# An mLSTM cell and a SwiGLU block in one kernel: first weights loaded earlier, words joined in place, and steps of the first group moved

## The chip, the cores and the metric

The kernel runs on one core of one Trainium2 chip. The metric is the device time of one launch in microseconds; the figure compared is the median of the timed runs. Block, piece and slot numbers count from 0.

## What is computed

The reference runs an mLSTM recurrence over 4 batches, 8 heads, 768 steps and head size 40, lays the heads of a token side by side, and puts the 3072 tokens of 320 values through a SwiGLU block with 1536 hidden values:

```python
for t in range(S):
    m_new = np.maximum(f_gate[:, :, t] + m, i_gate[:, :, t])
    f_stab = np.exp(f_gate[:, :, t] + m - m_new)
    i_stab = np.exp(i_gate[:, :, t] - m_new)
    C = f_stab * C + i_stab * outer(v_t, k_t)
    n = f_stab * n + i_stab * k_t
    y[:, :, t] = sigmoid(o_gate_t) * (C @ q_t) / max(|n . q_t|, 1)
x = y.transpose(0, 2, 1, 3).reshape(B * S, H * D)
g = x @ w_gate
out = (g * sigmoid(g) * (x @ w_val)) @ w_out
```

Inputs are float32, except that the three weight matrices come as float64 and are turned into float32 words on the chip.

## The kernel before

**Groups.** The 768 steps are cut into six groups of 128, for all 32 heads at once. For each group the recurrence is done in its chunked form (scores of q and k, weighed by gate factors, plus a state carried from 64 steps to 64 steps), and its 512 token rows (4 batches of 128) then go through the block: twelve hidden blocks of 128 values (`hidden`, L594 to L605, ten float32 matmuls each, into two PSUM banks of the tag "gen"; ScalarE takes the Silu of one, VectorE multiplies by the other), then the output projection (`project_all`, L618, for group 0, `project`, L612, for the others).

**The order is written out by hand.** The kernel runs under a manual schedule: each engine executes its instructions in the order in which the code emits them. The recurrence of group n+1 is put between the hidden blocks of group n, by the table `slots` (L671 for group 0) and, for group 0, the table `after` (L689) between the twelve steps of the projection. A slot's functions are emitted after the hidden block with its number.

**The first group** (L520 to L562) is done ahead of everything, in one piece of 128 steps per head: gate factors by matmuls into PSUM (`first_mask`, `first_inputs`, `first_maxima`), transposes of k and q (`first_turn`), scores, `first_own` and `first_x` per batch, `first_gate` (times the sigmoid of the output gates, `sig`), `first_seam` (transposes of the token rows, then copies into `xT`), `first_state`. Heads come in two halves, P = 0 and 1. `burn` (L422) issues matmuls on constant data whose result nobody reads.

**Weights.** `PIECES` cuts them into ten pieces: 0 and 1 hold hidden blocks 0 and 1, pieces 2 to 6 two hidden blocks each, pieces 7 to 9 the output matrix. `piece_load` (L136) loads the words of w_gate into partitions 0 to 63 through SP's queue (the gate half) and those of w_val into partitions 64 to 127 through ScalarE's queue (the val half). Pieces 0, 1, 4 and 5 share two buffers `raw`; pieces 2 and 6 use the end of `h_sb`, piece 3 the space of `wo_sb`. `convert(j)` (L206) makes float32 words of block j in three steps: `scale` (two ScalarE multiplications, into `top` and `low`), `join` (two VectorE operations, into `both`), `rounded` (an integer add of `both` and `low` into the weights' place, on GpSimd or VectorE). `top`, `low` and `both` have one buffer each. `ahead` (L668) says which block is converted behind which hidden block: m+2 behind m.

**Queues.** SP issues nearly all loads, ScalarE the first gate rows (L127, L129, L130) and the val halves. A transfer waits on its issuing engine for the buffers that it writes, and for the earlier transfer whose completion semaphore it takes over: eight such semaphores go round in the order of issue. What stands behind it on that engine waits too.

**Gate factors of the later groups.** `late_sums` and `late_maxima` (L271, L278) scan all later steps at once, `decay_rows` and `decay` prepare the decay factors, `late_turns` transposes the gate rows; `late_maxima` also writes `M_dram`, which `weights_load` (L400) spreads into `w_sb`. For a group `weights_sub`, `weights_mask` (GpSimd) and `weights_exp` make the factors, `do_scores` and `do_weigh` the weighed scores, `do_add` and `do_state` the two new states, `do_attend` and `do_gather` the outputs, `do_divide` and `seam` the rows for the block.

**PSUM.** Two tags of four banks each go round: "gen" (`first_y`, hidden blocks, projection) and "cell" (all else, the burns among it). A new tile waits until the readers of the bank's last tile are done.

Of the kernel before, what the change touches and what calls it, by code (L numbers as in the profile page):

```python
# [11 lines left out]
I32 = mybir.dt.int32  # L12
U32 = mybir.dt.uint32
AF = mybir.ActivationFunctionType
ALU = mybir.AluOpType
# [3 lines left out]
L = 128  # L19
# [5 lines left out]
def kernel(  # L25
# [18 lines left out]
    nc = tc.nc  # L44
# [12 lines left out]
    NKC = DM // HP  # L57
    UH = BH // 2
    UA = UH // 2
    NH = NFC + 1  # L60
# [10 lines left out]
    conv = early_scope.enter_context(tc.tile_pool(name="conv", bufs=2))  # L71

    def flat(t):
        return t.rearrange("p c t -> p (c t)")

    def bank(name, tag="cell"):
        return psum.tile([128, 512], F32, name=name, tag=tag)
# [7 lines left out]
    k_sb = const.tile([128, BH, DP], F32)  # L85
    q_sb = const.tile([128, BH, DP], F32)
    v_sb = const.tile([128, BH, D1], F32)
    o_sb = const.tile([128, BH, D], F32)
# [9 lines left out]
    h_sb = const.tile([128, NH, TW], F32)  # L98
# [7 lines left out]
    f_sb = early.tile([BH, NS - 2, SUB], F32)  # L106
    i_sb = early.tile([BH, NS - 2, SUB], F32)
# [4 lines left out]
    def load(dst, a, c, P):  # L112
        nc.sync.dma_start(out=dst[:, heads(P), 0:D], in_=tokens(a, c, P))
# [7 lines left out]
    def gate_rows(a):  # L121
        return a.rearrange("b h s -> (b h) s")
# [3 lines left out]

    nc.scalar.dma_start(out=f0, in_=spread_rows(f_gate))  # L127
    nc.sync.dma_start(out=i0, in_=spread_rows(i_gate))
    nc.scalar.dma_start(out=flat(f_sb), in_=gate_rows(f_gate)[:, L:])  # L129
    nc.scalar.dma_start(out=flat(i_sb), in_=gate_rows(i_gate)[:, L:])  # L130


    raws = {}
# [2 lines left out]
    def piece_load(p, home=None):  # L136
        kind, m, n = PIECES[p]
        if kind == "gv":
            a, d = NKC, n * 128
            src = [(slice(i * HP, (i + 1) * HP), w[:, m * 128:(m + n) * 128].rearrange("(c p) f -> p c f", p=HP))  # L140
                   for i, w in enumerate((moe_w_gate, moe_w_val))]
            queues = (nc.sync, nc.scalar)
        else:
            a, d = n, DM
            src = [(slice(0, 128), moe_w_out[m * 128:(m + n) * 128].rearrange("(a p) d -> p a d", p=128))]
            queues = (nc.sync,)
        if src[0][1].dtype == F32:
            for r, w in src:
                if kind == "o":
                    nc.sync.dma_start(out=wo_sb[r, m:m + n, :], in_=w)  # L150
                else:
                    for x in range(n):
                        nc.sync.dma_start(out=wgv_sb[r, m + x], in_=w[:, :, ts(x, 128)])
            return
        if home is None:
            raw = conv.tile([128, 4 * NKC * 128], U32, name="raw")
        else:
            raw = home.rearrange("p a t -> p (a t)").bitcast(U32)
        raw = raw[:, 0:2 * a * d]
        for (r, w), queue in zip(src, queues):  # L160
            queue.dma_start(out=raw[r].rearrange("p (a d) -> p a d", a=a), in_=w.bitcast(U32))
        words = raw.rearrange("p (a d two) -> p a d two", two=2, a=a)
        raws[p] = (words[:, :, :, 0], words[:, :, :, 1])
        split(p)


    blocks = {}
# [13 lines left out]
    def scale(j):  # L181
        if j in blocks:
            lo, hi, dst = blocks[j]
            a, d = hi.shape[1], hi.shape[2]
            top = conv.tile([128, NKC * 128], F32, name="top", bufs=1).rearrange("p (a d) -> p a d", a=a)
            nc.scalar.mul(top, hi.bitcast(F32), 2.0 ** -112)  # L186
            low = conv.tile([128, NKC * 128], I32, name="low", bufs=1).rearrange("p (a d) -> p a d", a=a)
            nc.scalar.mul(low, lo, 2.0 ** -29)
            blocks[j] = (low, top.bitcast(U32), dst)

    def join(j):
        if j in blocks:
            lo, top, dst = blocks[j]
            a = dst.shape[1]
            both = conv.tile([128, NKC * 128], U32, name="both", bufs=1).rearrange("p (a d) -> p a d", a=a)
            nc.vector.tensor_scalar(both, top, scalar1=3, scalar2=None, op0=ALU.logical_shift_left)  # L196
            nc.vector.scalar_tensor_tensor(both, in0=top, scalar=0x80000000, in1=both, op0=ALU.bitwise_and,  # L197
                                           op1=ALU.bitwise_or)
            blocks[j] = (lo, both, dst)

    def rounded(j, eng=None):
        if j in blocks:
            lo, both, dst = blocks.pop(j)
            (eng or nc.gpsimd).tensor_tensor(dst.bitcast(I32), both.bitcast(I32), lo, op=ALU.add)  # L204

    def convert(j, eng=None):  # L206
        scale(j)
# [5 lines left out]
        load(q_sb, q, 0, P)  # L213
        load(v_sb, v, 0, P)
    load(o_sb, o_gate, 0, 0)
    load(o_sb, o_gate, 0, 1)


    junk = early.tile([128, 512], BF16)
# [198 lines left out]
    def sig(P):  # L418
        nc.scalar.activation(o_sb[:, heads(P)], o_sb[:, heads(P)], AF.Sigmoid)


    def burn(n):  # L422
        t = bank("burn")
        for _ in range(n):
            nc.tensor.matmul(t, lhsT=junk[:, 0:128], rhs=junk, start=True, stop=True)  # L425

# [3 lines left out]
    A, V, G = nc.scalar, nc.vector, nc.gpsimd  # L430
# [52 lines left out]
    def first_own(u):  # L483
        first_y[u] = bank("first_y", "gen")[:, 0:H * D1].rearrange("p (h d) -> p h d", d=D1)
        for h in range(H):
            nc.tensor.matmul(first_y[u][:, h, :], lhsT=W0[:, u * H + h, :], rhs=v_sb[:, u * H + h, :], start=True, stop=True)  # L486

    def first_x(u):
        y = first_y.pop(u)
        den = work.tile([128, UH, 1], F32, name="den")[:, 0:H]  # L490
        nc.vector.tensor_scalar(den, y[:, :, D:], scalar1=1.0, scalar2=None, op0=ALU.max)
        nc.vector.scalar_tensor_tensor(den, in0=y[:, :, D:], scalar=-1.0, in1=den, op0=ALU.mult, op1=ALU.max)
        nc.vector.reciprocal(den, den)
        nc.vector.tensor_tensor(x_sb[:, u, 0:DM].rearrange("p (h d) -> p h d", d=D), y[:, :, 0:D],
                                den.to_broadcast([128, H, D]), op=ALU.mult)

    def first_gate(P):
        for u in (2 * P, 2 * P + 1):
            x = x_sb[:, u, 0:DM].rearrange("p (h d) -> p h d", d=D)
            nc.vector.tensor_tensor(x, x, o_sb[:, u * H:(u + 1) * H], op=ALU.mult)  # L500
        nc.gpsimd.tensor_copy(x_sb[:, 2 * P:2 * P + 2, DM:], x_sb[:, 2 * P:2 * P + 2, 0:HP])
# [9 lines left out]
    def first_seam(P, engs):  # L511
        for c, eng in zip(range(0, NKC, 2), engs):
            cs = range(c, min(c + 2, NKC))
            tp = bank("tp_x")[:, 0:len(cs) * 2 * L].rearrange("p (c u s) -> p c u s", u=2, s=L)
            for w in cs:
                for b in range(2):
                    nc.tensor.transpose(tp[:, w - c, b, :], x_sb[:, 2 * P + b, ds(PAIRS[w][0] * HP, 2 * HP)], ident)  # L517
            copy(eng, xT(0)[:, c:c + len(cs), 2 * P * L:(2 * P + 2) * L].rearrange("p c (u s) -> p c u s", u=2), tp)
# [14 lines left out]
    first_x(0)  # L533
    first_turn(1, q_sb, qT, (A, V))
    piece_load(0)
    piece_load(1)
    first_own(1)
    first_values(1)
    first_x(1)
    first_scores(1)  # L540
    sig(0)
    sig(1)
    piece_load(2, h_sb[:, NH - NKC:])
    piece_load(3, wo_sb)
    burn(3)
    first_own(2)
    first_own(3)
    first_gate(0)
    first_x(2)
    first_x(3)  # L550
    first_gate(1)
    first_seam(0, (A, V, A))
    scale(0)
    piece_load(4)
    burn(5)
    join(0)
    first_seam(1, (A, A, A))
    rounded(0, V)
    first_state(0, A)
    convert(1)  # L560
    piece_load(5)
# [98 lines left out]
    def load_all(dst, a, n):  # L660
        for P in range(2):
            load(dst, a, n, P)

    run = lambda f, *a: (lambda: f(*a))
# [4 lines left out]
    ahead[8] = [10, 11]  # L669
    ahead[9] = []  # L670
    slots = {  # L671
        0: [run(first_state, 1, A), run(load_all, k_sb, k, 1), run(load_all, q_sb, q, 1), run(late_maxima)],
        1: [run(decay_rows), run(piece_load, 6, h_sb[:, NH - NKC:])],
        2: [run(late_turns), run(weights_load, 1)],
        3: [run(decay), run(load_all, v_sb, v, 1)],
        6: [run(turn, 0, (A, A), (A, V)), run(piece_load, 7)],
        7: [run(turn, 1, (A, A), (A, V)), run(weights_sub, 1, 0), run(weights_sub, 1, 1), run(weights_mask, 0),
            run(weights_mask, 1)],
        8: [run(weights_exp, 0), run(weights_exp, 1), run(weigh_values, G, 0), run(weigh_values, G, 1),
            run(piece_load, 8)],  # L680
        9: [run(do_scores), run(do_weigh, 0), run(load_all, o_sb, o_gate, 1)],
        10: [run(do_weigh, 1), run(do_add), run(do_state, 2, 0), run(do_state, 2, 1)],
        11: [run(do_attend, 1, 0), run(do_gather, 1, 0, False), run(piece_load, 9)],
    }
    for m in range(NFC):
# [26 lines left out]
    for g in range(1, NG):  # L712
        n, f = g + 1, g + 2
# [64 lines left out]
```

## Time and profile before

| | |
|---|---|
| timed runs, us | 577.21, 577.31, 579.02; median 577.31 |
| the profiled execution, us | 579.26 |
| its span, us | 577.5 |
| mean granted TensorE clock | 0.993 |
| TensorE busy, us | 567.9 |
| hidden blocks (L599), busy us | 322.2 in 1440 records |
| VectorE, ScalarE, GpSimd busy, us | 211.7, 151.0, 102.4 |
| moved by DMA, MB | 37.85 |

The profile is of one execution. A float32 matmul is recorded as two passes, so a hidden block of ten matmuls shows as x20. A view by lines gives groups of instructions with their mean duration; the timeline gives start, length, engine, line, tile and, in brackets, the engine's idle time before it with what released it; the chain of waits is followed back from the last instruction of a window; a view by stretches gives busy time per engine, then the granted clock, the share of the DMA engines and GB/s. Matmuls are pipelined and their ends modelled, so a wait inside a row of matmuls can show as a longer row. L numbers are lines of the kernel before.

### The profile page before, as it was taken

What the parts mean: (1) busy time and instruction counts of PE and PEld (TensorE: products, weight loads), DVE (VectorE), ACT (ScalarE), POOL (GpSimd) and SP (SyncE); (2) the same over time, 40 slices, a digit from 0 to 9 for tenths busy, and PEclk for the clock granted to TensorE, in tenths of its full rate; (3) what the DMA queues carried; (4) which work ended last, traced back from release to release, by engine and by line L of the source; (5) the groups of instructions that cost most, each with busy time, mean ns of one, the idle gap of its engine ahead of it and who ended that gap; (6) DMA issues with size and microseconds to landing.
All of it is one profiled execution on the core that took longest, in us unless ns stands there. A gap on an engine that the chain in (4) does not pass through costs nothing.

```text
span 577.5 us, 12169 instructions
## 1 busy us (share of the span) xinstructions
PE 567.9 (98%) x5407; PEld 332.0 (57%) x5407; DVE 211.7 (37%) x378; ACT 151.0 (26%) x237; POOL 102.4 (18%) x101
## 2 busy tenths in 40 slices
PE   9998998999999999999999999999999999999997
PEld 4955454765655676455576555567555567544475
DVE  5776595860325600234620224630223630011100
ACT  3366554427210223201115210114311010011100
POOL 2132345463001141001132001232001110000000
PEclk9999998999999999999999999999999999999999
DMA  9999992494141800313620304450000000000000
GB/s 126 182 283 175 177 252 93 86 148 93 25 48 24 144 23 24 47 24 48 112 43 33 48 1 56 78 92 23 12 2 2 3 1 24 23 1 0 1 23 23
DMA packets 129915, 37.85 MB, mean 66 GB/s; under 512 B 120424, under 2 KB 125032, under 8 KB 129864
## 3 DMA queue, kind: packets, MB, share of 16 engines
q1 hardware_dynamic: 127284, 32.92, 33.0%
q10 hardware_dynamic: 2580, 4.16, 3.3%
q8 instruction: 42, 0.69, 0.5%
q14 instruction: 9, 0.07, 0.0%
HBM read 33.06 MB, written 4.01 MB: 64 GB/s over the span
## 4 chain that ended last, share of the span: by engine, by line
PE 91%; DMA 3%; ACT 3%; DVE 1%; issue 1%; POOL 0%; ACTq 0%; DVEq 0%; POOLq 0%
PE gv_ps L599 49%; PE o_ps L615 23%; PE o_ps L622 4%; DMA raw<-in_moe_w_val_dram 3%; PE inter L349 2%; PE intra L354 2%; PE add L330 2%; PE tp_kq L294 1%; PE sp L309 1%; PE first_y L486 1%; PE tp_x L395 1%; PE burn L425 1%; PE tp_x L517 1%; PE tp_kq L465 1%; PE sp L475 1%
## 5 line engine op out<-in xcount | busy, mean ns | idle before, releaser
L599 PE MATMUL gv_ps<-xT,wgv_sb 64*128 64x512 f32 x1440 | 322.2, 596 | 1.8 <-POOL wgv_sb L204 1.8
L599 PEld LDWEIGHTS gv_ps<-xT,wgv_sb 64*128 64x128 f32 x1440 | 139.6, 188 | 154.9 <-issue 150.2
L605 DVE TENSOR_TENSOR h_sb<-sg,gv_ps 128x512 f32<-128x512 f32 x72 | 49.5, 687 | 302.5 <-ACT sg L604 287.3
L615 PE MATMUL o_ps<-wo_sb,h_sb 128*128 128x320 f32 x480 | 130.5, 433 | 0.0
L615 PEld LDWEIGHTS o_ps<-wo_sb,h_sb 128*128 128x128 f32 x480 | 90.8, 190 | 38.2 <-issue 0.8
L604 ACT ACTIVATE sg<-gv_ps 128x512 f32<-128x512 f32 x72 | 43.0, 598 | 262.2 <-PE gv_ps L599 262.1
L339 POOL TENSOR_TENSOR C<-C,dec 128x328 f32<-128x328 f32 x20 | 14.5, 737 | 164.0 <-DVE C L341 164.0
L609 ACT COPY z_sb<-o_ps 128x320 f32<-128x320 f32 x24 | 10.2, 426 | 114.1 <-PE o_ps L615 102.7
L412 POOL TENSOR_SCALAR_AFFINE_SELECT w_sb<-w_sb 64x1024 f32<-64x1024 f32 x20 | 28.2, 1408 | 27.0 <-DVE w_sb L407 26.0
L622 PE MATMUL o_ps<-wo_sb,h_sb 128*128 128x320 f32 x96 | 26.9, 437 | 0.0
L375 POOL TENSOR_TENSOR o_sb<-o_sb,y_sb 128x640 f32<-128x640 f32 x10 | 14.2, 1428 | 48.6 <-DVE y_sb L366 48.6
L622 PEld LDWEIGHTS o_ps<-wo_sb,h_sb 128*128 128x128 f32 x96 | 17.9, 190 | 7.2
L366 DVE TENSOR_TENSOR y_sb<-y_sb,intra 64x328 f32<-64x328 f32 x40 | 19.7, 493 | 1.1
L319 POOL TENSOR_TENSOR vw_sb<-v_sb,w_sb 128x656 f32<-128x656 f32 x10 | 12.8, 1305 | 32.2 <-issue 32.2
L204 POOL TENSOR_TENSOR wgv_sb<-both,low 128x640 int32<-128x640 int32 x8 | 13.4, 1670 | 25.4 <-DVE both L197 25.4
L197 DVE SCALAR_TENSOR_TENSOR both<-top,both 128x640 uint32<-128x640 uint32 x18 | 15.7, 871 | 0.6
L349 PEld LDWEIGHTS inter<-C,qT 64*64 64x64 f32 x640 | 10.2, 134 | 7.3 <-issue 6.8
L196 DVE TENSOR_SCALAR both<-top 128x640 uint32<-128x640 uint32 x18 | 10.5, 581 | 9.3 <-ACT top L186 7.4
L330 PEld LDWEIGHTS add<-vw_sb,k_sb 64*64 64x64 f32 x640 | 10.5, 136 | 5.7 <-issue 4.9
L341 DVE TENSOR_TENSOR C<-C,add 128x328 f32<-128x328 f32 x20 | 9.9, 494 | 9.5 <-POOL C L339 9.3
L204 POOL TENSOR_TENSOR wo_sb<-both,low 128x640 int32<-128x640 int32 x6 | 10.2, 1700 | 17.4 <-DVE both L197 13.9
L407 DVE TENSOR_TENSOR w_sb<-g_T,w_sb 128x1024 f32<-128x1024 f32 x10 | 13.1, 1349 | 0.0
(120 smaller groups left out, 385.1 us busy)
## 6 DMA issues: line engine op xcount, KB each, us to landing
w_sb<-M_dram SPq DMA_DIRECT2D x10, 512.0 KB, 6.5
k_sb<-in_k_dram SPq DMA_DIRECT2D x12, 320.0 KB, 6.4
q_sb<-in_q_dram SPq DMA_DIRECT2D x12, 320.0 KB, 4.0
v_sb<-in_v_dram SPq DMA_DIRECT2D x12, 320.0 KB, 6.1
o_sb<-in_o_gate_dram SPq DMA_DIRECT2D x12, 320.0 KB, 6.8
raw<-in_moe_w_out_dram SPq DMA_DIRECT2D x3, 1280.0 KB, 7.2
out_dram<-z_sb SPq DMA_DIRECT2D x24, 160.0 KB, 1.8
h_sb<-in_moe_w_gate_dram SPq DMA_DIRECT2D x2, 640.0 KB, 9.0
```

The source lines that it names most:

```text
L197: nc.vector.scalar_tensor_tensor(both, in0=top, scalar=0x80000000, in1=both, op0=ALU.bitwise_and, op1=ALU.bitwise_or)
L204: (eng or nc.gpsimd).tensor_tensor(dst.bitcast(I32), both.bitcast(I32), lo, op=ALU.add)
L330: nc.tensor.matmul(ps[i][half(two), a, :], lhsT=k_sb[half(i), h, :], rhs=vw_sb[half(i), h, :], start=True, stop=True)
L339: nc.gpsimd.tensor_tensor(state(s + 1)[:, a], state(s)[:, a], dec[:, s - 2, a].unsqueeze(2).to_broadcast([128, UA, D1]), op=ALU.mult)
L349: nc.tensor.matmul(inter[two][half(i), a, :], lhsT=qT[half(two), P * UA + a, half(i)], rhs=state(2 * n + i)[half(two), P * UA + a, :], sta ...
L366: nc.vector.tensor_tensor(t, t, intra[i][half(c)], op=ALU.add)
L412: nc.gpsimd.affine_select(w, w, compare_op=ALU.is_ge, fill=NEG, base=0, pattern=[[0, UH], [1, SUB]], channel_multiplier=-1)
L599: nc.tensor.matmul(ps[i], lhsT=wgv_sb[half(i), m, PAIRS[kc][i], :], rhs=x[half(i), kc, :], start=(kc == 0), stop=(kc == NKC - 1))
L604: nc.scalar.activation(sg, ps[0], AF.Silu)
L605: nc.vector.tensor_tensor(hid(g, m), sg, ps[1], op=ALU.mult)
L615: nc.tensor.matmul(p, lhsT=hid(g, m)[:, ts(u, L)], rhs=wo_sb[:, m, :], start=(m == 0), stop=(m == NFC - 1))
L622: nc.tensor.matmul(ps[u], lhsT=hid(g, m)[:, ts(u, L)], rhs=wo_sb[:, m, :], start=(m == 0), stop=(m == NFC - 1))
```

## The change

- The rows of the later gates (`f_sb`, `i_sb`) are no longer loaded at the start, but on ScalarE's queue behind pieces 0 and 1.
- The second half of the first output gates (`o_sb`) is loaded behind piece 0 and not ahead of it.
- `join` writes its words into the weights' own place and `rounded` adds there; the tile `both` is gone, and `low` has two buffers.
- Block 0 is converted earlier and in three places: `scale` between the two sigmoids, `join` between the third and fourth `first_x`, `rounded` (now on GpSimd) behind the fourth.
- Between the two `first_seam` stand eight burns in a bank of "gen", where there were five in a bank of "cell"; the first copy of the second `first_seam` goes to VectorE.
- `late_maxima` moves behind hidden block 1, `decay_rows` behind block 2, `late_turns` behind 3, `decay` behind 4, the two `turn` behind blocks 5 and 6; the v loads move one slot ahead; both `do_weigh` stand behind block 9.

```diff
-    nc.scalar.dma_start(out=flat(f_sb), in_=gate_rows(f_gate)[:, L:])
-    nc.scalar.dma_start(out=flat(i_sb), in_=gate_rows(i_gate)[:, L:])
...
-            low = conv.tile([128, NKC * 128], I32, name="low", bufs=1).rearrange("p (a d) -> p a d", a=a)
+            low = conv.tile([128, NKC * 128], I32, name="low").rearrange("p (a d) -> p a d", a=a)
...
-            a = dst.shape[1]
-            both = conv.tile([128, NKC * 128], U32, name="both", bufs=1).rearrange("p (a d) -> p a d", a=a)
+            both = dst.bitcast(U32)
             nc.vector.tensor_scalar(both, top, scalar1=3, scalar2=None, op0=ALU.logical_shift_left)
...
-            blocks[j] = (lo, both, dst)
+            blocks[j] = (lo, dst.bitcast(I32))
...
-            (eng or nc.gpsimd).tensor_tensor(dst.bitcast(I32), both.bitcast(I32), lo, op=ALU.add)
+            (eng or nc.gpsimd).tensor_tensor(dst, dst, lo, op=ALU.add)
...
     load(o_sb, o_gate, 0, 0)
-    load(o_sb, o_gate, 0, 1)
...
-    def burn(n):
-        t = bank("burn")
+    def burn(n, tag="cell"):
+        t = bank("burn", tag)
...
     piece_load(0)
+    load(o_sb, o_gate, 0, 1)
     piece_load(1)
+    nc.scalar.dma_start(out=flat(f_sb), in_=gate_rows(f_gate)[:, L:])
+    nc.scalar.dma_start(out=flat(i_sb), in_=gate_rows(i_gate)[:, L:])
     first_own(1)
     first_values(1)
     first_x(1)
     first_scores(1)
     sig(0)
-    sig(1)
     piece_load(2, h_sb[:, NH - NKC:])
     piece_load(3, wo_sb)
+    scale(0)
+    sig(1)
     burn(3)
     first_own(2)
     first_own(3)
     first_gate(0)
     first_x(2)
+    join(0)
     first_x(3)
+    rounded(0)
     first_gate(1)
     first_seam(0, (A, V, A))
-    scale(0)
+    burn(8, "gen")
     piece_load(4)
-    burn(5)
-    join(0)
-    first_seam(1, (A, A, A))
-    rounded(0, V)
+    first_seam(1, (V, A, A))
...
-        0: [run(first_state, 1, A), run(load_all, k_sb, k, 1), run(load_all, q_sb, q, 1), run(late_maxima)],
-        1: [run(decay_rows), run(piece_load, 6, h_sb[:, NH - NKC:])],
-        2: [run(late_turns), run(weights_load, 1)],
-        3: [run(decay), run(load_all, v_sb, v, 1)],
-        6: [run(turn, 0, (A, A), (A, V)), run(piece_load, 7)],
-        7: [run(turn, 1, (A, A), (A, V)), run(weights_sub, 1, 0), run(weights_sub, 1, 1), run(weights_mask, 0),
-            run(weights_mask, 1)],
+        0: [run(first_state, 1, A), run(load_all, k_sb, k, 1), run(load_all, q_sb, q, 1)],
+        1: [run(late_maxima), run(piece_load, 6, h_sb[:, NH - NKC:])],
+        2: [run(weights_load, 1), run(load_all, v_sb, v, 1), run(decay_rows)],
+        3: [run(late_turns)],
+        4: [run(decay)],
+        5: [run(turn, 0, (A, A), (A, V))],
+        6: [run(turn, 1, (A, A), (A, V)), run(piece_load, 7)],
+        7: [run(weights_sub, 1, 0), run(weights_sub, 1, 1), run(weights_mask, 0), run(weights_mask, 1)],
...
-        9: [run(do_scores), run(do_weigh, 0), run(load_all, o_sb, o_gate, 1)],
-        10: [run(do_weigh, 1), run(do_add), run(do_state, 2, 0), run(do_state, 2, 1)],
+        9: [run(do_scores), run(do_weigh, 0), run(do_weigh, 1), run(load_all, o_sb, o_gate, 1)],
+        10: [run(do_add), run(do_state, 2, 0), run(do_state, 2, 1)],
```

More of the change, by code (lines that the diff above doesn't have):

```diff
@@ L198, in join @@
                                            op1=ALU.bitwise_or)
-            blocks[j] = (lo, both, dst)
+            blocks[j] = (lo, dst.bitcast(I32))
     def rounded(j, eng=None):
         if j in blocks:
-            lo, both, dst = blocks.pop(j)
-            (eng or nc.gpsimd).tensor_tensor(dst.bitcast(I32), both.bitcast(I32), lo, op=ALU.add)
+            lo, dst = blocks.pop(j)
+            (eng or nc.gpsimd).tensor_tensor(dst, dst, lo, op=ALU.add)
     def convert(j, eng=None):
```

## The prediction

> **What bounds the kernel now.** I read the busy shares first, then the chain that ended last, TensorE's timeline, the waits and the DMA view, all for the first 134 us: after that the diff touches nothing.
>
> ```profile
> PE 567.9 (98%) x5407; PEld 332.0 (57%) x5407; DVE 211.7 (37%) x378; ACT 151.0 (26%) x237; POOL 102.4 (18%) x101
> ```
>
> TensorE is busy 98% of the span, so a change can win only what TensorE idles, burns or does slowly. TensorE's timeline has it (start, length, line, idle before and its releaser):
>
> ```profile
> 31.02 1.31 PE L517 MATMUL tp_x<-ident,x_sb 128*128 128x128 f32 x10
> 33.33 4.56 PE L599 MATMUL gv_ps<-xT,wgv_sb 64*128 64x512 f32 x20
> ...
> 38.88 8.85 PE L599 MATMUL gv_ps<-xT,wgv_sb 64*128 64x512 f32 x40
> ...
> 49.46 4.74 PE L599 MATMUL gv_ps<-xT,wgv_sb 64*128 64x512 f32 x20 [0.99 <-POOL wgv_sb L204]
> ...
> 55.47 13.15 PE L599 MATMUL gv_ps<-xT,wgv_sb 64*128 64x512 f32 x60 [0.80 <-POOL wgv_sb L204]
> ...
> 85.53 5.71 PE L599 MATMUL gv_ps<-xT,wgv_sb 64*128 64x512 f32 x20
> 91.17 1.34 PE L330 MATMUL add<-vw_sb,k_sb 64*64 64x41 f32 x64
> 93.92 0.28 PE L330 MATMUL add<-vw_sb,k_sb 64*64 64x41 f32 x2 [1.41 <-DVE w_sb L316]
> 94.52 1.36 PE L330 MATMUL add<-vw_sb,k_sb 64*64 64x41 f32 x62 [0.32 <-DVE w_sb L316]
> 95.81 5.97 PE L599 MATMUL gv_ps<-xT,wgv_sb 64*128 64x512 f32 x20
> 101.71 1.14 PE L349 MATMUL inter<-C,qT 64*64 64x41 f32 x64
> ```
>
> One hidden block (20 records, two passes of ten matmuls) takes 4.35 to 4.4 us unhindered. To be had: 0.99 and 0.80 us waiting for converted words of blocks 3 and 4, about 1.3 us in block 10 (5.71), 1.73 us in the second `add`, and 1.6 us in block 11 (5.97), which the clock explains:
>
> ```profile
> 96.00:98.00 2.00, 2.00 (x6) 0.97 (x8) 0.99 (x2) 0.00 (x0) 1.39 (x3) 0.50 0.88 209
> ```
>
> The last three numbers are TensorE's granted clock (0.50), DMA share, GB/s: half clock for some 3.4 us after the thin stretch around 93. Together 6.4 us. The chain from 24 to 60 us says what the early waits hang on:
>
> ```profile
> 35.29 15.40 DMA raw<-in_moe_w_val_dram
> ...
> 50.76 0.60 ACTq L161
> ...
> 51.49 0.80 ACT top L186
> ...
> 52.38 0.51 DVE both L196
> ...
> 53.88 1.55 POOL wgv_sb L204
> ...
> 55.47 4.56 PE gv_ps L599 x19
> ```
>
> ScalarE's own transfer (piece 6, val half) waits for the semaphore of piece 5's val half, and everything behind it on ScalarE waits along. Such waits decide the changed kernel too; the DMA view gives the landing that I need:
>
> ```profile
> wo_sb<-in_moe_w_gate_dram SPq DMA_DIRECT2D x1, 640.0 KB, 15.8
> ```
>
> Piece 3's gate half, issued at 22.00, landed at 37.8. By issue plus landing, pieces 0 and 1's gate halves landed at 28.1 and 29.8.
>
> **What the Trainium skill says.** "TensorE: Matmul & The Clock Gate", part 1, describes a free-running activity window of about 3.4 us, after which the clock is halved or restored; the trace agrees (0.50 from 27.0 to about 30.4 and from about 95.3 to 98.6). "DMA: Bandwidth & Descriptors", "Issuing engines are not separate DMA queues", says that all queues run on the same 16 engines; the trace agrees: the DMA engines are saturated from 3 to 62 us, so reordering moves one landing at another's expense. "SBUF — State Buffer", "SBUF: two separate sides", says that VectorE with two SBUF inputs and GpSimd lock each other out; in the trace GpSimd's join add takes 2.59 us at 36.10 beside VectorE's sums, 1.53 alone.
>
> **Part by part.**
>
> *In-place join, two low tiles.* Same operations, same shapes (0.49, 0.83, 1.54 us): nothing. ScalarE's `low` no longer waits for GpSimd (6.0 us of idle in the waits view), which is on the path only where ScalarE is: there it brings `sg` of blocks 8 and 9 forward by 0.8 us. The add of block 0's words goes from VectorE (0.83) to GpSimd (1.54), one `xT` copy from ScalarE to VectorE (0.68): both end before ScalarE's copies do, so nothing.
>
> *Loads moved.* The two early loads (160 KB) go from ahead of everything to ScalarE after piece 1, and piece 0's gate half goes ahead of the second output gates. Beside the early loads SP's issue of `v_sb` took 3.13 us against 2.15 for its like, so I take 0.8 us of advance for all that follows on SP (bounds 0.6 and 1.0). But the eight DMA semaphores go round in another order. The built program has ScalarE wait, before issuing, for these landings: `i_sb` for piece 0's gate half, piece 2 for the second output gates, piece 3 for **piece 1's gate half**, piece 4 for **piece 3's gate half**. Before, none of these held it. Behind the first queue the sigmoid table and `sig(0)`; behind piece 3 queue `scale(0)` and `sig(1)`, for which VectorE waits in `join(0)`, ahead of `first_x(3)` and the second gate; behind piece 4 queue two of the three copies of the second `xT` half, the state copy and `scale(1)`.
>
> Piece 1's gate half: 29.8 - 0.8 = 29.0. Then piece 3's issue 0.6, `top` 0.8, join 1.4, first_x 1.1, gate 0.9, transposes 1.35, `add` 1.05: block 0 starts near 36.2 instead of 33.33. Eight burns instead of five (+1.0 us) lie inside this wait; if it weren't there they would cost 1 us.
>
> Piece 3's gate half: 37.8, less 0.8, less 1.8 because it shared the engines from 30.6 to 35.2 with val halves that are now issued later (none of that to half of those 4.6 us: 0 to 2.3), plus 0.5 for the displaced 160 KB: 35.7. I keep 34.0 and 37.8 as ends. From there: issue 0.7, copies and state copy 1.3, `top` 0.8, join 1.4, GpSimd 2.6 (beside the sums, as before): block 1's words are ready 6.8 us later, at 42.5; it started at 38.88.
>
> Much of these 3.6 us is taken up again. `late_maxima` is now behind block 1, so block 3's words no longer wait for it (0.99 gone). From block 1's start: three blocks 13.2, transposes of the gates 0.8, and block 4 starts at 42.5 + 14.1 = 56.6. ScalarE keeps pace: block 1 ends at 46.9, exp done about 5 us later (sg 0.6, product 0.7, maxima 2.8, exp 0.8), then piece 6's issue 0.6, scales 1.5, table 1.3, sg 0.6, product 0.7 frees block 2's bank at 56.6. Before, block 4 started at 55.47 with `decay` (0.53) done: now **1.7 us late**. This holds if piece 5's val half lands by 52: the bytes ahead of it are the same, so I take its 50.7. On SP the write of `M_dram` stays behind the k and q loads (57.98 before, some 2 us later now), so moving the maxima costs it nothing; `w_sb` landed by 72, some 2 later now, against a need near 78; the v loads stand behind it as before. The `turn`s, one slot earlier, find q landed: before at 60.7 and 64.5, now some 2 us later, against 66 and 71.
>
> *Late part*, counted from block 8's start (74.77 before). Block 10 waits as before for VectorE's product of block 8 (subtractions and two blocks' joins beside GpSimd's masks). `sg(9)` ends at 13.85, product at 14.55, then all four weighings to 17.1: both `add`s find their banks, 16.8 to 18.8, no idle, so block 11 runs at full clock to 23.2 (before: 26.9). Here 3.7 us are won. Part goes back: `join(12)` now follows the weighings, so GpSimd starts the state products at 20.05 instead of 19.45; they take 4.65 as before, then join 1.3, product 0.7, gathers 0.9 and 2.05, `intra` 1.0, which ends at 30.7. Before it ended at 33.3. VectorE is late next. **Won: 2.6 us** (2.0 if the thin stretch meets the clock's window, 3.7 if VectorE holds nothing). Then o_ps covers the divides (2.6 us of slack before `seam`).
>
> Sum: +1.7 - 2.6 = -0.9 us. The profiled execution took 579.26 us with a span of 577.5: 578.4 and 576.6 after. The median of the timed runs, 577.31, is what I carry it to: **576.4**.
>
> **Rivals.** *Weights abreast*: with weights on both queues from 22 us on, they move 0.34 MB/us together, one queue alone 0.20 (slices of the DMA view). Piece 3 lands at 34.0, block 1's words are ready at 40.8; piece 5's landing at 50.7 and the 4.8 us behind it then decide: block 4 at 55.5, 0.6 late. 577.3 + 0.6 - 2.6 = 575.3; with 3.7 won, 574.2. For it: SP issues piece 1 earlier. Against: before, the two queues took turns from 21.6 to 30.6.
>
> *The semaphore order costs more than it brings* (slower): piece 3 lands at 37.8 as before, the bytes ahead being the same; block 1 starts at 44.6, 3.8 us late at block 4. TensorE stands about 3 us in this stretch, and as after 93 a window at half clock follows: 1.6 us. +3.8 + 1.6 - 2.6 = +2.8: 580.1. It decides from a landing of 36.6 on; without the half clock it is slower by 0.3% from 38.3.
>
> *No late gain*: VectorE, still behind its joins, holds `add` or `attend` anyway, and only 0.5 us is won: +1.7 - 0.5: 578.5.
>
> **Numbers.** 0.3% is 1.73 us, about what a measurement of this kernel can tell from no change: faster is below 575.6, slower above 579.0. Forecast 0.36 (own range 575.0 to 578.2; 0.11 of it faster, 0.23 same, 0.02 slower); weights abreast 0.32 (0.30 faster, 0.02 same); semaphore order 0.22 (0.20 slower, 0.02 same); no late gain 0.10 (0.06 same, 0.04 slower). Faster 0.41, same 0.33, slower 0.26. The range 574.0 to 579.9 leaves out about half of the slower case and a little below.
>
> **What would show it.** ScalarE's queue with piece 4's issue at the landing of piece 3's gate half, block 0 broken in the middle, block 1 at 42 to 43; no 0.99 before block 3; `add` without idle, block 11 at 4.4 us, granted clock 1.00 there; waits of `intra` on VectorE. I am wrong if ScalarE is not held before the second `xT` copies, or if block 11 stays near 6 us.

## The result

The changed kernel is slower. Median of the timed runs: 581.9 us (581.55 to 582.91, 4 runs) against 577.26 us (576.91 to 579.02, 4 runs) for the kernel before, ratio 1.0074, 95% interval 1.0055 to 1.0093. The forecast was 576.4 with a range up to 579.9. The profiled execution took 582.04 us with a span of 580.3 us; that of before took 579.26 with 577.5. Ratios, here and below, leave out executions in a slow state, more than 1.5% above the fastest of the same kernel (only two of e3's 22), and need not be the quotient of the medians shown.

A repetition on another chip (experiment e5) gave 581.42 against 579.45, ratio 1.0031 (1.0017 to 1.0044). The changed kernel takes nearly the same time in every execution; the kernel before doesn't. Over the 182 executions of it that the three sets of experiments brought, it took 576.5 to 583.2 us, median 579.06, mostly along its mean granted clock: median 577.64 at 0.996 (46 executions), 579.05 at 0.993 and 0.994 (76), 581.53 at 0.988 (18). The 13 at 0.997 don't fit, with a median of 579.89, so the clock isn't all of it. The loss is 2.0 us in the larger set and 4.6 us in the first one. Executions of the kernel before at 0.996 would nearly account for that, but of the first four only the profiled one has its clock on record (0.993).

The busy shares of the changed kernel's page, TensorE first:

```profile
PE 569.4 (98%) x5410; PEld 331.6 (57%) x5410; DVE 212.9 (37%) x378; ACT 149.6 (26%) x236; POOL 104.0 (18%) x102
```

TensorE is busy 1.5 us more (567.9 before) in a span that is 2.8 us longer; the shares tell no more than that. The lines of its timeline that answer to those of before (start, length, line, tile, idle before):

```profile
29.01 2.27 PE L421 MATMUL burn<-junk 128*128 128x512 bf16 x8
35.36 1.87 PE L513 MATMUL tp_x<-ident,x_sb 128*128 128x128 f32 x10 [4.08 <-DVE x_sb L496]
37.16 1.94 PE L504 MATMUL add<-vw_sb,k_sb 128*64 128x41 f32 x32
39.03 6.73 PE L598 MATMUL gv_ps<-xT,wgv_sb 64*128 64x512 f32 x20
45.69 1.13 PE L504 MATMUL add<-vw_sb,k_sb 128*64 128x41 f32 x32
46.75 13.15 PE L598 MATMUL gv_ps<-xT,wgv_sb 64*128 64x512 f32 x60
...
60.56 4.56 PE L598 MATMUL gv_ps<-xT,wgv_sb 64*128 64x512 f32 x20
...
76.24 13.10 PE L598 MATMUL gv_ps<-xT,wgv_sb 64*128 64x512 f32 x60
...
97.38 2.08 PE L326 MATMUL add<-vw_sb,k_sb 64*64 64x41 f32 x128
99.38 4.56 PE L598 MATMUL gv_ps<-xT,wgv_sb 64*128 64x512 f32 x20
```

Block 0 starts at 39.03 (before 33.33), block 1 at 46.75 (38.88), block 4 at 60.56 (55.47), and block 8, the second of the group at 76.24, at 80.6 (74.77): 5.8 us late. Then the late gain: the second weighed `add` runs without its 1.73 us of idle, and block 11 takes 4.56 instead of 5.97. From the start of block 8 to the second output products (111.21, before 108.08) it takes 30.6 us instead of 33.3. That is 2.7 us won. Between the two traces 5.8 - 2.7 = 3.1 us are left, and the spans differ by 2.8.

ScalarE's queue shows what happened early (ACTq are its own transfers, in brackets its idle time):

```profile
30.47 0.60 ACTq L159 DMA_DIRECT2D wo_sb<-in_moe_w_val_dram  x1
31.12 0.77 ACT L184 ACTIVATE top<-raw 128x640 f32<-128x640 f32 x1 [6.51 <-DMA raw<-in_moe_w_gate_dram]
31.79 0.77 ACT L186 ACTIVATE low<-raw 128x640 int32<-128x640 uint32 x1
32.46 0.73 ACT L415 ACTIVATE o_sb<-o_sb 128x640 f32<-128x640 f32 x1
...
38.89 0.60 ACTq L159 DMA_DIRECT2D raw<-in_moe_w_val_dram  x1
39.54 0.86 ACT L117 COPY xT<-tp_x 128x512 f32<-128x512 f32 x2 [5.60 <-PE add L504]
```

Piece 3's val half (the `wo_sb` transfer) is issued at 30.47, when piece 1's gate half has landed; behind it stand the scaling of block 0 and the second sigmoid. VectorE's `join(0)` waits for this scaling, and the second gate, which the second transposes need, stands behind the join:

```profile
31.92 0.49 DVE L193 TENSOR_SCALAR wgv_sb<-top 128x640 uint32<-128x640 uint32 x1 [5.35 <-ACT top L184]
```

Piece 4's val half is issued at 38.89, when piece 3's gate half has landed; behind it stand the `xT` copies and the scaling of block 1. The idle of 5.60 names TensorE's `add`, but the copies need only the transposes, which ended at 37.2; they began when the transfer had been issued (38.89 + 0.60).

TensorE idles for 4.1 us meanwhile, and then works at half speed. Stretches of 2 us; the last three columns are granted clock, DMA share and GB/s:

```profile
38.00:40.00 2.00, 2.00 (x24) 1.45 (x22) 0.00 (x0) 0.46 (x1) 0.00 (x0) 0.50 1.05 201
40.00:42.00 2.00, 2.00 (x8) 0.93 (x6) 0.53 (x2) 2.00 (x5) 0.00 (x0) 0.50 1.03 237
...
96.00:98.00 2.00, 2.00 (x50) 1.00 (x46) 2.00 (x5) 0.65 (x2) 0.00 (x0) 1.00 0.00 0
```

The half clock behind block 10 (96 to 98) is gone, as forecast; one around block 0 has come. What the DMA view says of piece 3's gate half in the changed kernel (the last number is the time from issue to landing):

```profile
wo_sb<-in_moe_w_gate_dram SPq DMA_DIRECT2D x1, 640.0 KB, 14.6
```

And SP's queue in the timeline, whose last line is its issue:

```profile
15.85 2.64 SPq L159 DMA_DIRECT2D raw<-in_moe_w_gate_dram  x1
18.53 0.60 SPq L113 DMA_DIRECT2D o_sb<-in_o_gate_dram  x1
19.18 4.21 SPq L159 DMA_DIRECT2D raw<-in_moe_w_gate_dram  x1
23.43 0.62 SPq L159 DMA_DIRECT2D h_sb<-in_moe_w_gate_dram  x1
24.18 0.59 SPq L159 DMA_DIRECT2D wo_sb<-in_moe_w_gate_dram  x1
```

It landed at 24.18 + 14.6 = 38.8, not at the forecast 35.7.

### The profile page after: what moved, and what is told of

The parts are those of the page before. It is cut to its first block, busy times and chain, and to the rows that moved or that the text cites. A ratio compares the mean times of both kernels' runs of the same rounds, so it can differ in the third digit from the quotient of the medians.

```text
span 580.3 us, 12162 instructions
## 1 busy us (share of the span) xinstructions
PE 569.4 (98%) x5410; PEld 331.6 (57%) x5410; DVE 212.9 (37%) x378; ACT 149.6 (26%) x236; POOL 104.0 (18%) x102
## 4 chain that ended last, share of the span: by engine, by line
PE 87%; SPq 3%; DVE 3%; DMA 2%; ACT 2%; issue 1%; POOL 1%; ACTq 0%; DVEq 0%
PE gv_ps L598 51%; PE o_ps L614 22%; PE o_ps L621 4%; SPq L113 3%; DMA raw<-in_moe_w_gate_dram 2%; PE intra L350 2%; PE inter L345 2%; PE tp_kq L290 1%; PE sp L305 1%; PE add L326 1%; PE tp_x L391 1%; DVE wgv_sb L194 1%; DVE wgv_sb L193 1%; PE add L504 1%; POOL C L335 0%
## 5 line engine op out<-in xcount | busy, mean ns | idle before, releaser
L598 PEld LDWEIGHTS gv_ps<-xT,wgv_sb 64*128 64x128 f32 x1440 | 138.2, 188 | 155.5 <-issue 152.5
L201 POOL TENSOR_TENSOR wgv_sb<-wgv_sb,low 128x640 int32<-128x640 int32 x9 | 14.9, 1655 | 33.5 <-DVE wgv_sb L194 25.9
L184 ACT ACTIVATE top<-raw 128x640 f32<-128x640 f32 x12 | 9.6, 800 | 17.9 <-DMA raw<-in_moe_w_gate_dram 6.5
L193 DVE TENSOR_SCALAR wgv_sb<-top 128x640 uint32<-128x640 uint32 x12 | 9.1, 757 | 13.7 <-ACT top L184 13.7
L201 POOL TENSOR_TENSOR wo_sb<-wo_sb,low 128x640 int32<-128x640 int32 x6 | 10.2, 1706 | 15.0 <-DVE wo_sb L194 10.4
L312 DVE TENSOR_TENSOR w_sb<-sp,w_sb 128x512 f32<-128x512 f32 x20 | 12.7, 682 | 0.0
```

Of the source, the lines that this page charges most:

```text
L201: (eng or nc.gpsimd).tensor_tensor(dst, dst, lo, op=ALU.add)
L598: nc.tensor.matmul(ps[i], lhsT=wgv_sb[half(i), m, PAIRS[kc][i], :], rhs=x[half(i), kc, :], start=(kc == 0), stop=(kc == NKC - 1))
```

## Theories and experiments

**Semaphore theory**: ScalarE is held at pieces 3 and 4 by completion semaphores, and what is lost is lost to the work that stands behind those two waits. **Rival, loads**: the new order of the transfers itself makes the bytes late. **Rival, conversion**: VectorE's `join(0)`, put ahead of the last `first_x` and the second gate, holds these. **Rival, half clock**: the clock behind the idle costs time of its own (e4). Medians below come with the ratio to the kernel before on the same chip; each set of four shares one chip.

### First set: order of the loads, and the half clock

e1, the later gate rows back at the start:

```diff
+    nc.scalar.dma_start(out=flat(f_sb), in_=gate_rows(f_gate)[:, L:])
+    nc.scalar.dma_start(out=flat(i_sb), in_=gate_rows(i_gate)[:, L:])
...
     piece_load(1)
-    nc.scalar.dma_start(out=flat(f_sb), in_=gate_rows(f_gate)[:, L:])
-    nc.scalar.dma_start(out=flat(i_sb), in_=gate_rows(i_gate)[:, L:])
```

> The changed kernel with the rows of the later gates loaded at the start again; the second output gates stay behind piece 0. This moves 160 KB of 37.85 MB and turns the eight semaphores by two places: ScalarE's piece 3 waits for piece 0's gate half instead of piece 1's, and piece 4 for piece 1's instead of piece 3's. Semaphore theory (the 4.1 us that TensorE idles ahead of block 0, and the half clock behind it, come from ScalarE being held at piece 3 until 30.5): piece 3 is issued by 28.5, block 0 starts at 34 to 35.5 at full clock (4.4 instead of 6.73), block 1 near 40 to 42, the time is 3 to 5 us below the changed kernel's 581.9: 577 to 579, or 575 with the whole late gain. Rival, order of the loads (the landings themselves are late, because SP's issues stand behind each other): piece 1 and 3 land as before or later, less than 1 us is won: 581 to 582. Rival, order of the conversion on VectorE: no change, 582.

Measured: 579.36 us (575.03 to 583.26, 22 runs), ratio 1.0001 (0.9979 to 1.0024). Block 0 came as the semaphore theory had it (34.52); block 1 (43.44) and the time did not.

e2, the second output gates back ahead of piece 0:

```diff
     load(o_sb, o_gate, 0, 0)
+    load(o_sb, o_gate, 0, 1)
...
     piece_load(0)
-    load(o_sb, o_gate, 0, 1)
```

> The changed kernel with the second output gates loaded ahead of piece 0 again; the rows of the later gates stay behind piece 1. Bytes in the old order but for the rows, yet the semaphores still make ScalarE's piece 3 wait for piece 1's gate half and piece 4 for piece 3's. Semaphore theory: little is won, block 0 still starts at 38 to 39.5 with a long idle ahead of it and half clock: 581 to 582.5. Rival, order of the loads: the second sigmoid and piece 1's landing come as before, block 0 by 36, 3 us won: 578 to 579. Rival, order of the conversion: 582.

Measured: 580.6 us (579.94 to 581.79, 22 runs), ratio 1.0036 (1.0023 to 1.0049).

e3, both moved back (the two diffs together):

> The changed kernel with both moved loads back in their old places; conversion, burns and slots as in the changed kernel. ScalarE's piece 3 then waits only for the second output gates (long landed), piece 4 for piece 1's gate half. Semaphore theory and loads theory alike: the early loss is gone, the late gain of 2.6 us stays: 574.5 to 575.5, faster than both kernels. Rival, order of the conversion on VectorE (join ahead of the last product and of the second gate) or the moved slots cause the early loss: 580 to 582.

Measured: 580.29 us (575.12 to 583.99, 22 runs), ratio 0.9993 (0.9969 to 1.0017): ten runs below 577.8, twelve above 580.2.

e4, more burns:

```diff
-    burn(8, "gen")
+    burn(22, "gen")
```

> The changed kernel with 22 burns instead of 8 between the two seams, so that TensorE works through the idle 31.3 to 35.4. Half clock as a cause of its own: the clock stays at 1.00 from 36 to 43, transposes, add and block 0 take 6.8 us together instead of 10.5; block 1 then starts when its words are ready (45.5 less about 1.5): 1.5 to 2.5 us won, 579.5 to 580.5. If the half clock only sits in time in which the words of block 1 are waited for anyway: 582, no change.

Measured: 581.24 us (580.34 to 582.47, 22 runs), ratio 1.0032 (1.0015 to 1.0048), like the changed kernel's own.

e2 speaks for the semaphores: old order of the output gates, same waits, nothing won that the intervals show (1.0036 against 1.0031 in e5). The trace has block 0 at 37.67 and block 1 at 44.76; the chain of waits to the latter goes through ScalarE's wait at piece 4:

```profile
21.16 16.84 DMA wo_sb<-in_moe_w_gate_dram
...
38.08 0.60 ACTq L159
...
39.92 0.69 ACT top L184
...
42.13 2.58 POOL wgv_sb L201
44.71 0.04 issue
44.76 1.55 PE gv_ps L598 x5
```

Issued 3 us earlier than in the changed kernel (21.16), piece 3's gate half still landed at 38.0.

e1 and e3 brought a surprise. With the semaphores turned, ScalarE issues pieces 2 and 3 at 20.6 and 22.6 (e1), and now these transfers compete with the ones that the first blocks need. In e1 piece 1's gate half landed at 36.7 instead of 30.4, and piece 4 waits for just that one; the copies behind it break block 0 in two. The second output gates landed at 30.5 instead of 27.9, and the second sigmoid waited for them (30.58), so part of e1's delay belongs to the rival *loads*. In e3's profiled execution (583.68 us) piece 0's gate half came at 31.8, and TensorE idled 6.6 us; no trace shows one of its ten executions below 577.8. First TensorE's timeline of e1, then a line of ScalarE's of e3:

```profile
34.52 1.99 PE L598 MATMUL gv_ps<-xT,wgv_sb 64*128 64x512 f32 x8
38.03 2.85 PE L598 MATMUL gv_ps<-xT,wgv_sb 64*128 64x512 f32 x12 [1.52 <-ACT xT L117]
```

```profile
31.82 0.78 ACT L186 ACTIVATE top<-raw 128x640 f32<-128x640 f32 x1 [9.49 <-DMA raw<-in_moe_w_gate_dram]
```

So undoing the loads is no sure cure: "faster than both" was wrong for e3's median, whose spread is 9 us. The waits that the change brought in also kept bytes back that were needed later.

The traces also say something on the rival *conversion*. In e1 `join(0)` has the same place on VectorE as in the changed kernel, but starts without a wait:

```profile
26.30 0.48 DVE L195 TENSOR_SCALAR wgv_sb<-top 128x640 uint32<-128x640 uint32 x1
```

In e3's trace it waits 6.63 us, for a scaling that waits for piece 0. So by these traces the new place of the join costs about its own 1.3 us of work, but it hands any delay of the scaling on to the second gate. No run moves the join alone; e7 and e10 move it together with ScalarE's work.

e4 didn't test quite what it was meant to: 22 burns ran at full clock in 4.91 us, 3.1 us of idle were left, and half clock followed from 35.6 to 39. But block 0 took 4.56 and the time didn't move: block 1 started at 46.15 after waiting 1.16 us for GpSimd's words. So the half clock of the changed kernel sits mostly in time that block 1's words take anyway.

### Second set: what stands behind the waits

e5, no edit:

> The changed kernel once more, without any edit, so that the others are compared with it on the same chip. All theories: 581 to 583, with a spread below 2 us (four runs before: 581.55 to 582.91), while the kernel before spreads over 6 us on this chip.

Measured: 581.42 us (581.05 to 582.17, 15 runs), ratio 1.0031 (1.0017 to 1.0044), the granted clock between 0.987 and 0.997. Its trace has less half clock than the first one (34.6 to 38, block 0 in 4.56), and the chain of waits to block 1 is then purely this:

```profile
25.36 12.98 DMA wo_sb<-in_moe_w_gate_dram
...
38.42 0.60 ACTq L159
...
39.55 0.38 ACT xT L117
39.92 0.34 ACT C L117
40.26 0.70 ACT top L184
...
41.52 0.83 DVE wgv_sb L194
...
42.48 2.59 POOL wgv_sb L201
45.07 0.04 issue
45.12 3.27 PE gv_ps L598 x13
```

From the landing at 38.34 to the ready words at 45.07 it takes 6.7 us; the prediction's sum for this was 6.8. It would also explain why the changed kernel hardly spreads: block 1 is pinned to a landing, and half clock before it costs little. That is argued, not shown.

e6, e2's edit, and piece 4 behind the conversion of block 1:

```diff
     burn(8, "gen")
-    piece_load(4)
     first_seam(1, (V, A, A))
     first_state(0, A)
     convert(1)
+    piece_load(4)
     piece_load(5)
```

> The changed kernel with the second output gates ahead of piece 0 (as in e2) and piece 4's load issued behind the conversion of block 1 and not ahead of the second seam. Nothing is left behind ScalarE's wait for piece 3's gate half. Semaphore theory: block 1's words no longer wait for piece 3's gate half (38.0 in e2); block 1 starts where block 0 and the add end, 43.2 to 43.5 instead of 44.76, or earlier if block 0 is earlier: 1.3 us below e2's 580.6, 579 to 579.6. Rival, landings: piece 1's words come late themselves, block 1 at 44.5 to 45: 580.6. Piece 4 comes later and holds block 6 or 7: 581 to 582.

Measured: 579.12 us (575.91 to 581.54, 14 runs), ratio 0.9988 (0.997 to 1.0007), against 1.0036 for e2: the time that the semaphore theory forecast. No wait for words is left ahead of block 1; in the profiled execution (580.5) a half clock from 34.7 to 41.5 keeps it at 45.21 all the same, now because block 0 itself is slow (6.34). With the pin gone, the spread is back.

e7, further:

```diff
     sig(0)
+    sig(1)
     piece_load(2, h_sb[:, NH - NKC:])
-    piece_load(3, wo_sb)
     scale(0)
-    sig(1)
+    piece_load(3, wo_sb)
...
     first_x(2)
-    join(0)
     first_x(3)
-    rounded(0)
     first_gate(1)
     first_seam(0, (A, V, A))
+    join(0)
+    rounded(0)
```

> As e6, and with the second sigmoid ahead of piece 2's load, the scaling of block 0 ahead of piece 3's, and VectorE's join of block 0 behind the second gate: the waits for semaphores stay, but nothing of the first two blocks stands behind them, and the second gate no longer waits for piece 0. Semaphore theory: second transposes by 30, block 0 at 32 to 34 at full clock, block 1 at 37.5 to 39.5, no half clock from 33 on; with the late gain 574 to 576. Rival, landings: the bytes of pieces 2 to 5 are late by as much as the first blocks are early, and TensorE idles ahead of blocks 2 to 5 instead: 577.5 to 580.

Measured: 578.01 us (575.65 to 580.85, 18 runs), ratio 0.9978 (0.9961 to 0.9996). In the trace block 0 starts at 34.19 and block 1 at 39.74, about as the semaphore theory had it (up to 34 and 39.5). The time is where the rival put it: later TensorE waits 1.38 us ahead of block 4.

e8, the kernel before with the slots of the changed one:

> The kernel before with only the slots of the changed one (later maxima, decay, turns, v loads, both weighings); the opening is the old one. The late gain of 2.6 us is all in the slots: block 11 at full clock, add without idle: 2 to 2.6 us below the kernel before on the same chip, with the same spread: ratio 0.9955 to 0.9965. And late maxima behind block 1 take 0.99 us of waiting off block 3: up to 1 us more. Rival, the late gain needs the join in place or the two low tiles: less than 1 us.

Measured: 580.58 us (577.71 to 582.67, 22 runs), ratio 1.0015 (1.0000 to 1.0030). Both expectations missed. The late stretch is shorter (31.5 instead of 33.3), but block 4 waits 1.56 us for its words and a half clock follows (6.35 for the block), so that block 8 starts at 76.2 instead of 74.8. In the median the slots alone bring no gain.

### Third set: loads against victims, and the late part

e9, the kernel before, one look:

> The kernel before once more, for a second trace of it: its times spread over 6 us and go with the mean granted clock (about 577 at 0.996, 578.5 at 0.994, 581.6 at 0.988), so that the one trace at hand (579.26, 0.993) may show a half clock that its faster executions do not have. If the half clock behind block 10 is a matter of phase, another trace may show the stretch from block 8 to the first gap-free output product shorter than 33.3 us, at about 31.7; the forecast gain of 2.6 us then was partly against an unlucky trace. If it is bound to the thin stretch in every execution: 33.3 again.

Measured: 580.41 us, granted clock 0.991. The stretch takes 34.6 us (74.82 to 109.42), more than in the first trace and not one of the two outcomes expected. TensorE's timeline:

```profile
93.97 0.41 PE L330 MATMUL add<-vw_sb,k_sb 64*64 64x41 f32 x2 [1.41 <-DVE w_sb L316]
94.57 1.94 PE L330 MATMUL add<-vw_sb,k_sb 64*64 64x41 f32 x62 [0.19 <-DVE w_sb L316]
96.44 6.67 PE L599 MATMUL gv_ps<-xT,wgv_sb 64*128 64x512 f32 x20
```

The half clock now lies over all of block 11. Its place and length change from execution to execution, and both traces at hand took longer than the median of their set.

e10, the changed kernel with its own order of loads, and only the victims moved: e7's diff and e6's move of piece 4, without e2's.

> The changed kernel with its own order of loads (second output gates behind piece 0, later gate rows behind piece 1), but with nothing of the first blocks behind ScalarE's waits: second sigmoid ahead of piece 2, scaling of block 0 ahead of piece 3, piece 4 behind the conversion of block 1, and the join of block 0 behind the second gate. Semaphore theory: what was lost was lost to what stood behind the waits, not to the order of the loads: block 0 at 33.5 to 35.5, block 1 within 1 us of e7's 39.7, 577.5 to 579, like e7's 578.0. Rival, order of the loads: the second output gates and piece 1 land later than in e7, block 0 at 36 or later, 580 to 581.5.

Measured: 577.98 us (576.5 to 579.84, 22 runs), ratio 0.9970 (0.9957 to 0.9984). This is the decisive run between semaphores and loads: all transfers are in the changed kernel's order (only piece 4's is issued later), the semaphores still make ScalarE wait, and 3.4 us of 581.4 are gone (medians of two sets; by the two ratios 3.5), as the semaphore theory forecast. What of this is due to the join's new place and what to ScalarE's work it doesn't tell. ScalarE's queue, then TensorE's timeline:

```profile
28.59 0.79 ACT L184 ACTIVATE top<-raw 128x640 f32<-128x640 f32 x1
...
30.60 0.60 ACTq L159 DMA_DIRECT2D wo_sb<-in_moe_w_val_dram  x1
31.24 0.86 ACT L117 COPY xT<-tp_x 128x512 f32<-128x512 f32 x2 [1.18 <-PE tp_x L513]
```

```profile
34.12 4.56 PE L598 MATMUL gv_ps<-xT,wgv_sb 64*128 64x512 f32 x20
38.62 1.13 PE L504 MATMUL add<-vw_sb,k_sb 128*64 128x41 f32 x32
39.68 4.56 PE L598 MATMUL gv_ps<-xT,wgv_sb 64*128 64x512 f32 x20
```

Piece 3 is issued at 30.60, as late as in the changed kernel (30.47), but the scaling of block 0 is done by then. Block 0 starts 4.9 us and block 1 7.1 us earlier than in the first trace of the changed kernel, 4.4 and 5.4 us earlier than in e5's. Part of it is given back: blocks 2 and 4 wait 1.00 and 1.90 us for words. The intervals of e10 and e7 overlap, so what the place of the second output gates is worth can't be seen here.

e11, e7 with the old slots and only the second weighing moved ahead:

> As e7, but with the old slots (later maxima behind block 0, decay, turns and v loads where they were), and of the slots only the second weighing moved ahead. My working said that the maxima behind block 1 give block 3 back 0.99 us and cost nothing later; e7's trace has block 4 waiting 1.4 us on the chain from the maxima instead. If the wait just moves: block 3 waits 0.5 to 1.0, block 4 less than 0.8, the time within 0.7 us of e7. If the late maxima cost: 0.7 to 1.5 us below e7's 578.0. The stretch from block 8 to the second output products stays at 30.6 us if both weighings alone make the late gain; 31 to 33 if the earlier turns are needed.

Measured: 578.22 us (576.0 to 579.16, 22 runs), ratio 0.9980 (0.9967 to 0.9993). The wait just moves, as expected, though it is longer than expected: block 3 waits 1.35 us, block 4 not at all. The late stretch takes 30.3 us (77.31 to 107.56) without the earlier turns.

e12, the kernel before with one edit:

```diff
-        9: [run(do_scores), run(do_weigh, 0), run(load_all, o_sb, o_gate, 1)],
-        10: [run(do_weigh, 1), run(do_add), run(do_state, 2, 0), run(do_state, 2, 1)],
+        9: [run(do_scores), run(do_weigh, 0), run(do_weigh, 1), run(load_all, o_sb, o_gate, 1)],
+        10: [run(do_add), run(do_state, 2, 0), run(do_state, 2, 1)],
```

> The kernel before with one edit: both weighings behind block 9. If they make the late gain: add without idle, the stretch from block 8 to the second output products 30.6 to 31 us instead of 33.3, 1 to 2.6 us below the kernel before (579.4 on the last chip): ratio 0.9955 to 0.998. Rival, the late gain needs the conversion's two low tiles, or the opening: the stretch 31.5 or more, ratio 0.998 to 1.001.

Measured: 578.23 us (576.4 to 581.81, 14 runs), ratio 0.9994 (0.9976 to 1.0013): inconclusive. The late stretch takes 31.2 us (75.95 to 107.12) at full clock, so in this trace one edit brings 2.1 of the 2.7 us. But in this execution block 3 waits 1.39 us and runs at half clock, and block 8 starts 1.2 us later than in the first trace of before.

## Why the prediction was wrong

**ScalarE's waits** were named rightly, with what stands behind each. The step that failed is "Piece 3's gate half: 37.8, less 0.8, less 1.8 ... plus 0.5 ...: 35.7". Measured: 38.8 and 38.3 in the two traces. Neither deduction shows. The 0.8 us of advance on SP was used up at once: piece 1's issue took 4.21 us (5.46 in e5; both first pieces together 2.32 before), so piece 3 was issued at 24.18, not at 21.2. And the issue time isn't what counts: issued at 21.16 (e2), 22.00 (before), 24.18 (after), 25.36 (e5) or 25.75 (e10), it landed at 38.0, 37.8, 38.8, 38.3 and 39.7. Against the 1.8 us stands e2: piece 3's val half was issued at 28.85 instead of 24.68, the gate half 0.8 us earlier, and the landing didn't move. Where the val halves of pieces 2 and 3 went out early, it landed later: at 43.0 in e1 (val halves at 20.6 and 22.6, gate half at 24.43). In the changed kernel the engines are full and move some 200 GB/s; that the bytes ahead are the same, as the rival said, fits this, but wasn't counted.

**Block 1.** From the landing on, the sum held (6.7 of 6.8 us): 42.5 + 2.6 = 45.1, the start in e5. In the first trace it is 46.75, because block 0, late and at half clock, ended later than the words were ready.

**Block 0** was forecast at 36.2 and came at 39.0 (38.5 in e5). Piece 1's gate half landed at 30.4 instead of 29.0, and the transposes and `add` ran partly at half clock and took 1.4 us longer; the forecast had full clock there. "A window at half clock follows" stood only in the rival.

**Late gain.** 2.6 us forecast, 2.7 us in the trace, by the way that was forecast (`add` without idle, block 11 at full clock). That the size agrees is in part luck: against e9's stretch of 34.6 us it would be 4.0, and without the 1.6 us of half clock in block 11 some 1.1 (an estimate from the first two traces). No median shows it alone (e8, e12). It was forecast against a trace with half clock behind block 10, and then carried to the median of runs: "The median of the timed runs, 577.31, is what I carry it to". That is the second step that failed. The profiled execution took 579.26 at a mean clock of 0.993; executions of before near 577 have 0.996 and more, so they can hardly all have had the half clock that was to be won. Of the 5.5 us between 576.4 and 581.9, 1.8 come from this step, and 3.6 lie between the profiled executions (578.4 forecast, 582.04 measured): there the term of +1.7 was 5.8.

**The maxima.** "Block 3's words no longer wait for it (0.99 gone)" holds for the changed kernel, but where the blocks aren't late, block 4 waits instead (1.38 us in e7, 1.90 in e10, 1.56 in e8; with the old slots, e11, it is block 3 with 1.35). In the changed kernel the late blocks hide this.

**The burns** cost nothing, as forecast; nor did they help (e4). The in-place join and the second low tile weren't tried alone. The rival *The semaphore order costs more than it brings* took place: landing at 38, block 1 at 44.6 (45.1 and 46.75 measured), half clock behind the idle. Its sum of +2.8 us, put to the profiled execution, gives 582.1 against 582.04; its total of 580.1 was short by the carrying to the median.

**Open** are what makes the executions of the kernel before differ by 6 us (their mean clock goes along with it only in part), what the join's place costs alone, and why SP's issue of piece 1 takes so long. How much late gain an execution of before at 0.996 has to give wasn't seen, since no trace is of one.

## What to carry to other kernels

When loads are reordered, list for each transfer which earlier one its completion semaphore waits for, and what stands behind it on its engine; don't take an earlier landing from an earlier issue (issued at 21.16 and 24.18, piece 3's gate half landed at 38.0 and 38.8). Undoing the order was no sure cure (e3: 0.9993, with a spread of 9 us); what helped was to move the needed work ahead of the waiting transfer (e10: 0.9970, faster than both kernels). And a gain that is read from a half clock in one trace is carried to that execution's time, not to a median.

## What was not expected of the hardware

- Taking ScalarE's wait away let pieces 2 and 3 compete, and piece 1's gate half came 6.3 us later (36.7 in e1 against 30.4). Here a wait had kept a landing early.
- Kernels in whose trace block 1 stands behind the landing of piece 3's gate half spread by 1.1 to 2.1 us (e5, e2, e4); the others by 3 to 9 us (e1, e3, e6, e7, e8, e10, e11, e12 and the kernel before). e1 is among these although the landing of piece 1 breaks its block 0, so a landing alone doesn't make the spread small.
- The same kernel had half clock from 26.4 to 29.8 and from 36.6 to 43.6 in one trace (582.04 us) and only from 34.6 to 38 in the other (581.14).
